# Moving the normalising steps by one step in an attention kernel on Trainium2, and giving its second head the values-in-the-array form

## The chip, the cores and the metric

The kernel runs on one core of one Trainium2 chip. The metric is device microseconds of one execution. The change is compared with the kernel before it, which took 1919.98 us (median of 3 runs, 1919.51 to 1921.93).

Engine names are those of the profile: PE is TensorE (PEld its weight loads), DVE is VectorE, ACT is ScalarE, POOL is GpSimd, SP is SyncE, which here issues DMAs.

## The reference, cut to what matters

```python
B, Sq, D = 1, 2048, 640;  H, Sk, Dh = 32, 2048, 192;  F = 1536
xn = layernorm(x)
q  = (xn @ wq) as 32 heads of 192
p  = softmax(q @ k_cache^T * Dh**-0.5)          # 2048 x 2048 for each head
s  = concat(p @ v_cache) @ wo
g  = silu((silu(xn @ w1) * (xn @ w3)) @ w2)
out = x + s * g
```

All operands are bf16. Almost all the work is attention: 32 heads, each with scores (contraction 192) and values (contraction 2048) for 2048 queries and 2048 keys.

## The kernel before, in words

**Heads, blocks, steps.** One head after another is computed. A head has four *blocks* of 512 queries (`qb` 0 to 3), a block has eight *steps* (`p` 0 to 7), and a step takes 256 keys (two tiles of 128). This text writes "step 3" for `p == 3`, and "block (3, 2)" for head 3, `qb` 2. `step` (line 755) writes one step into the program:

1. `scores` (549): matmuls into one PSUM tile `st` of 128x1024 floats. There are two such tiles (`ps_st`, line 183); the projections use them too.
2. `weights` (566): one ACT exponential reads `st` and writes half of `pT`, bf16. A `pT` tile holds two steps, and its pool `pp` has three buffers (line 176). A block needs four `pT` tiles, so the tile of steps 6 and 7 takes the buffer of steps 0 and 1 of the same block, and the tile of steps 0 and 1 of the next block that of steps 2 and 3.
3. Value matmuls, which lag behind: `parts` is a list from which each step pops some. From step 3 on, five parts stay in the list (line 777), so each step runs two parts of the step but one before it and the first part (`high(0)`) of the step just before it.
4. In step 1, `extra` (1010): the projection of the same block of the next head's queries (`project_chunk`, 366, PE), and its two casts out of PSUM, `qF` and `qA` (line 386).
5. `do_chores` (732) at the end of the step: the delayed pieces whose time has come on a step counter, in the order in which they were put there; then at most one piece of `lazy`, in the steps that `slots` names.

Program order is the order of each engine's queue for everything that is pinned, and all of this is.

**Two forms of a head.** Heads 2 to 30 are *quads* (`in_quads`, 158): every matmul is 64x64, four at a time in the four quarters of the array. In the values (`values_quads`, 634), the 64x64 of `vt` is the loaded operand and `pT` (512 queries) streams, so that the output comes out with its channels on the partitions. Heads 0, 1 and 31 use `values` (610) instead: `pT` is loaded and `vt`, with a column of ones, streams, 193 wide. There the row sums of the softmax come out of the matmul, and `evict` (589) adds and normalises.

**Row sums of a quad head.** They are made on DVE (`row_sums`, 676), from all four `pT` tiles of a block:
- `fours`: the sum of two `pT` tiles (128x2048). It is due two counts after steps 3 and 7, which puts it at the end of step 4 of the block and of step 0 of the next. It is called the *second-half sum* when it stands in step 0 (it sums steps 4 to 7 of the block before) and the *first-half sum* when it stands in step 4 (it sums steps 0 to 3).
- `join`, `fold`, `ends`: due at the end of step 2 of the next block; the last writes `e`, which a DMA turns into `eT`.
- `turned_sums` (710): due 6 counts after `ends` (line 701), that is at the end of step 0, two blocks after the one that it belongs to. Five DVE instructions: reduce `eT` to `rs`, its reciprocal, and three that normalise `ox` into `ostage`; `staged` then issues a store from the SP queue when both heads of a pair are in.

**Output additions.** The outputs of a block lie in four PSUM banks. `evict_quads` (660) runs in step 1 of the next block, after the exponential: ACT copies one bank (`oa`, 665), DVE adds the other (`ot`, 666), twice, and a DMA turns `ot` into `ox`. These additions free the banks.

**Bound steps.** The exponential needs a bound `nb` for each head. `fold_keys` (415: three DVE reductions over the keys), `column_lengths` (430: two DVE pieces of squares and one of roots) and `head_bound` (459: three small DVE operations and a POOL reduction over the partitions) are put into `lazy` in step 3 of a block (1025 to 1034) and taken out one by one in the steps of `slots` (736).

**SwiGLU.** In odd heads, `swiglu_chunk` (528) gives one tanh on ACT and two DVE operations for each block.

Behind head 31 lie the FFN output and the output projection, about 290 us, which the diff doesn't touch.

Of the kernel before, what the change touches and what calls it, by code (L numbers as in the profile page):

```python
# [30 lines left out]
def _kernel_impl(ctx, tc, A_x, A_k_cache, A_v_cache, A_wq, A_wo, B_w1, B_w3, B_w2, out):  # L31
    nc = tc.nc
    _, SQ, D = A_x.shape
    _, H, SK, dh = A_k_cache.shape
# [5 lines left out]
    NQB = SQ // 512  # L40
# [48 lines left out]
    def load_weights(h):  # L89
        keep = pin if h <= 3 else (lambda x: x)  # L90
        wsel = B_w1 if h % 2 == 0 else B_w3
        m = h // 2
        parts = ((A_wq[:, h * DH:h * DH + P], 0, 0, P), (wsel[:, m * PGW:(m + 1) * PGW], 1, 0, PGW),
                 (A_wq[:, h * DH + P:(h + 1) * DH], 1, PGW, P))
        if h == 0:
            wq = lnx.tile([P, 2, DC, P], BF16, name="wq0")

            def piece(part):
                w, t, c0, c1 = part
                pin(nc.sync.dma_start(out=wq[:, t, :, c0:c1], in_=w.rearrange("(c p) d -> p c d", p=P)))  # L100
            return dict(wq=wq, pieces=[lambda part=part: piece(part) for part in parts])
        else:
            wq = wqp.tile([P, 2 * DC, P], BF16, tag="wq")
            for w, t, c0, c1 in parts:
                keep(nc.gpsimd.dma_start(out=wq[ROWS[t], :, c0:c1], in_=w.rearrange("(s p) d -> p s d", p=DT)))
        return dict(wq=wq)
# [49 lines left out]
            set_ones(L)  # L156

    def in_quads(h):
        return 1 < h < H - 1

    def load_ahead(h, qb):
        if qb == 0:
            loads[h] = load_weights(h)
        elif qb == 1:
            loads[h].update(load_keys(h, hold=True))
            loads[h]["rest"].pop(0)()
        elif qb == 2:
            while loads[h]["rest"]:
                loads[h]["rest"].pop(0)()
            copy_keys(h, loads[h])  # L170
# [3 lines left out]
    with ExitStack() as actx:  # L174
# [495 lines left out]
        def later(wait, f, *a):  # L670
            chores.append((clock[0] + wait, f, a))

        def add(out, a, b):
            pin(nc.vector.tensor_tensor(out=out, in0=a, in1=b, op=ALU.add))  # L674

        def row_sums(hd, qb, p, w):
            sm = hd["sums"]

            def fours():
                t = aq["tree"].tile([P, 2, 1024], BF16, tag="tree", name="tree")  # L680
                a, b = sm["w"]
                sm["w"] = []
                add(t[:], a[:], b[:])
                sm["t"].append(t)

            def join():
                a, b = sm["t"]
                add(a[:], a[:], b[:])
                sm["t"].pop()

            def fold():
                t = sm["t"][0]
                add(t[:, 0, :], t[:, 0, :], t[:, 1, :])

            def ends():
                t = sm["t"].pop()[:, 0, :]
                e = aq["two"].tile([P, 512], BF16, tag="e", name="e")
                add(e[:], t[:, 0:512], t[:, 512:1024])
                eT = aq["two"].tile([P, 4, P], BF16, tag="eT", name="eT")
                pin(nc.sync.dma_start_transpose(out=eT[:], in_=e[:]))  # L700
                later(6 if in_quads(hd["h"] + 1) or qb < NQB - 1 else 9, turned_sums, hd, qb, eT)

            sm["w"].append(w)
            if p % 4 == 3:
                later(2, fours)
            if p == NPAIR - 1:
                for f in (join, fold, ends):
                    later(4, f)
# [23 lines left out]
        def do_chores(h, qb, p):  # L732
            for c in [c for c in chores if c[0] <= clock[0]]:
                chores.remove(c)
                c[1](*c[2])
            slots = (5,) if h % 2 and h > 1 else (5, 6) if h > 1 and qb % 2 == 0 else (5, 6, 7)
            if p in slots and lazy and lazy[0][0] <= clock[0]:
                _, f, a = lazy.pop(0)
                f(*a)
# [211 lines left out]
        def load_last():  # L951
            w = wqp.tile([P, 2 * DC, P], BF16, tag="wq", name="wl")
            for r, src in zip(ROWS, (B_w1, B_w3)):
                nc.gpsimd.dma_start(out=w[r, :, :], in_=src[:, FPIG:FPIG + P].rearrange("(s p) d -> p s d", p=DT))
            last.update(w=w, g=qp.tile([P, SQ], BF16, tag="qA", name="gl"), u=qfp.tile([P, SQ], BF16, tag="qF", name="ul"))
# [22 lines left out]
        for h in range(1, H):  # L978
            if h >= H // 2 and ffn_w_loads:
                ffn_w_loads.pop(0)()  # L980
            if h == 1:
                loads[3] = load_weights(3)
                while loads[2]["rest"]:
                    loads[2]["rest"].pop(0)()
            elif h + 2 == H:
                load_last()
            if h + 1 < H:
                start_head(h + 1)
            hd = heads[h]
            hd.update(sums=dict(w=[], t=[]), ox={})  # L990
            if h == 1:
                lengths = [2]
                todo = []
            elif h + 1 < H:
                lengths = [] if h % 2 else [h + 1] + [h + 2] * (h + 2 < H)
                todo = [h + 1]
            else:
                lengths = todo = []
            chunks = [[0], [1], [2], [3]] if h + 1 < H else [[0, 1], [2, 3], [], []]
            gated = []  # L1000
            for qb in range(NQB):
                post = []
                if (h, qb) == (H - 1, 2):
                    while chores:
                        clock[0] += 1
                        do_chores(h, qb, 2)
                    astack.close()
                    acc["hTp"] = fstack.enter_context(tc.tile_pool(name="hTp", bufs=2, side="right"))

                def extra():  # L1010
                    if h % 2 == 1:
                        for c in chunks[qb]:
                            gate = swiglu_chunk(h // 2, heads[h - 1]["qF"], hd["qF"], c)
                            gated.append(gate if hd["quads"] else gate())
                    quads = before["quads"] if qb == 0 else hd["quads"]
                    if h + 1 < H:
                        post.append(project_chunk(h + 1, qb, quads=quads, cast_low=nc.scalar.copy if hd["quads"] else None))
                    else:
                        post.append(hidden_last(qb, quads))

                for p in range(NPAIR):
                    step(hd, qb, p, extra if p == 1 else None)
                    if p == 4 and 1 < h < H - 2:
                        load_ahead(h + 2, qb)
                    if p == 3 and (h, qb) != (1, 0):
                        keys = todo or ([2] if (h, qb) == (1, 1) else [])
                        for k in keys:
                            lazy.extend(fold_keys(k))
                        for k in lengths[:1] if qb % 2 == 0 or h == 1 else []:
                            lazy.extend(column_lengths(k))  # L1030
                            lengths = lengths[1:]
                        for k in keys:
                            lazy.append((0, head_bound, (k,)))
                        todo = []
                    if (h, qb, p) == (1, 0, 7):
                        copy_keys(2, heads[2]["L"])
                        loads[3].update(load_keys(3))
                    if (h, qb, p) == (1, 2, 7):
                        copy_keys(3, loads[3])
                    if h + 1 < H:  # L1040
                        if p == 3 and gated:
                            if hd["quads"]:
                                later(1, lambda f=gated.pop(0): gated.append(f()))
                            later(3, lambda: gated.pop(0)())
                    else:
                        if p > 4 and gated:
                            gated.pop(0)()
                        if p == 3:
                            gated.append(post.pop()())
            while lazy:  # L1050
                _, f, a = lazy.pop(0)
                f(*a)
                assert 0, "late"
            heads.pop(h - 1, None)
            before["quads"] = hd["quads"]
# [143 lines left out]
    with ExitStack() as dctx:  # L1199
# [32 lines left out]
        todo = [lambda qb=qb, j=j: parts.append(load_part(pools, qb, j)) for qb in range(LB) for j in range(4)][3:]  # L1232
# [177 lines left out]
```

## Time and profile before

| what | value |
|---|---|
| median of 3 runs | 1919.98 us (1919.51 to 1921.93) |
| the profiled execution, its own time | 1919.95 us |
| span of that execution in the profile | 1918.4 us |
| PE busy | 1911.2 us, 100% of the span |
| DVE busy | 1426.2 us, 74% |
| ACT busy | 1382.2 us, 72% |
| POOL busy | 160.0 us, 8% |
| granted TensorE clock | 1.0 |

The profile has a page (busy time of each engine, the span in 40 slices, the chain of work that ended last, the costliest groups of instructions) and a trace that can be asked for a timeline, for waits, and for busy time in chosen windows. In a timeline a row gives the start and the length in us, engine, line of the kernel, operation, tiles written and read, how many instructions were merged into the row, and in brackets the idle time before it and what ended it. Ends of matmuls are modelled: each shows about 0.38 us, while the next group of four starts 0.216 us after it. So PE's busy share says little; starts say more.

### The profile page before, as it was taken

What the parts mean: (1) busy time and instruction counts of PE and PEld (TensorE: products, weight loads), DVE (VectorE), ACT (ScalarE), POOL (GpSimd) and SP (SyncE); (2) the same over time, 40 slices, a digit from 0 to 9 for tenths busy, and PEclk for the clock granted to TensorE, in tenths of its full rate; (3) what the DMA queues carried; (4) which work ended last, traced back from release to release, by engine and by line L of the source; (5) the groups of instructions that cost most, each with busy time, mean ns of one, the idle gap of its engine ahead of it and who ended that gap; (6) DMA issues with size and microseconds to landing.
All of it is one profiled execution on the core that took longest, in us unless ns stands there. A gap on an engine that the chain in (4) does not pass through costs nothing.

```text
span 1918.4 us, 68912 instructions
## 1 busy us (share of the span) xinstructions
PE 1911.2 (100%) x30919; PEld 1201.9 (63%) x30919; DVE 1426.2 (74%) x2558; ACT 1382.2 (72%) x1521; POOL 160.0 (8%) x308
## 2 busy tenths in 40 slices
PE   9999999999999999999999999999999999999999
PEld 5665555566666666666666666666666666454456
DVE  8658888888888888888888888888888885521111
ACT  7778888888888888888888888888888887210000
POOL 3300100000000000010000000101000000000000
PEclk9999999999999999999999999999999999999999
DMA  8735656666665656666656565656666634937673
GB/s 170 151 73 101 138 108 129 115 122 113 119 127 113 127 104 126 108 126 119 129 105 133 103 129 101 138 96 139 106 131 113 124 60 125 272 82 156 159 151 76
DMA packets 598955, 235.86 MB, mean 123 GB/s; under 512 B 523312, under 2 KB 588304, under 8 KB 598656
## 3 DMA queue, kind: packets, MB, share of 16 engines
q1 hardware_dynamic: 585712, 201.80, 54.1%
q0 software_dynamic: 8256, 24.58, 4.9%
q8 instruction: 242, 3.96, 0.9%
q10 hardware_dynamic: 4688, 5.05, 0.9%
q14 instruction: 57, 0.47, 0.1%
HBM read 54.26 MB, written 31.98 MB: 45 GB/s over the span
## 4 chain that ended last, share of the span: by engine, by line
PE 98%; DMA 0%; DVE 0%; SPq 0%; ACT 0%; POOL 0%; issue 0%
PE st L562 34%; PE obank L641 31%; PE ps L363 14%; PE ps_s L1154 8%; PE obank L621 3%; PE ps_s L1110 3%; PE ps_f L1174 2%; PE ps_gu L941 1%; PE ps_f L1190 1%; PE ps L348 0%; DMA eT<-e 0%; DMA KT<-in_A_k_cache_dram 0%; DVE tree L674 0%; SPq L116 0%; PE ps_gu L348 0%; SPq L100 0%
## 5 line engine op out<-in xcount | busy, mean ns | idle before, releaser
L570 ACT ACTIVATE pT<-st,nb 128x1024 bf16<-128x1024 f32 x1016 | 1125.2, 1113 | 188.7 <-PE st L562 152.5
L641 PE MATMUL obank<-pT,vt 64*64 64x512 bf16 x11136 | 778.4, 376 | 0.2 <-DVE ot L666 0.2
L641 PEld LDWEIGHTS <-vt 64*64 64x64 bf16 x11136 | 397.5, 107 | 221.6 <-issue 0.8
L562 PE MATMUL st<-qS,KM 64*64 64x512 bf16 (+1 forms) x1951 | 410.4, 376 | 0.4 <-POOL qS L393 0.4
L562 PE MATMUL st<-qA,KT 64*64 64x512 bf16 (+1 forms) x1951 | 410.3, 376 | 0.0
L562 PE MATMUL st<-qD,KT 64*64 64x512 bf16 (+1 forms) x1951 | 410.3, 376 | 0.0
L562 PE MATMUL st<-qA,KM 64*64 64x512 bf16 (+1 forms) x1951 | 391.3, 376 | 0.0
L562 PE MATMUL st<-qS,KT 64*64 64x512 bf16 (+1 forms) x1951 | 391.2, 376 | 0.1
L562 PE MATMUL st<-qF,KT 64*64 64x512 bf16 (+1 forms) x1951 | 391.2, 376 | 0.0
L562 PEld LDWEIGHTS <-KT 64*64 64x64 bf16 (+1 forms) x7808 | 274.9, 106 | 150.8 <-issue 0.6
L363 PE MATMUL ps<-xnT,wq 64*64 64x512 bf16 (+1 forms) x2390 | 291.1, 376 | 0.0
L363 PE MATMUL ps<-xnS,wq 64*64 64x512 bf16 (+1 forms) x2390 | 287.9, 376 | 0.0
L674 DVE TENSOR_TENSOR tree<-pT,pT 128x2048 bf16<-128x2048 bf16 x232 | 282.7, 1218 | 3.2 <-ACT pT L570 3.2
L363 PEld LDWEIGHTS <-wq 64*64 64x64 bf16 (+1 forms) x4780 | 167.4, 107 | 98.0
L674 DVE TENSOR_TENSOR tree<-tree 128x2048 bf16<-128x2048 bf16 x232 | 221.2, 954 | 4.0
L666 DVE TENSOR_TENSOR ot<-oa,obank 128x512 bf16<-128x512 f32 x232 | 148.9, 683 | 84.7 <-ACT oa L665 84.2
L562 PEld LDWEIGHTS <-KM 64*64 64x64 bf16 (+1 forms) x3904 | 144.8, 106 | 62.9 <-issue 1.2
L1154 PE MATMUL ps_s<-oT,wo_sb 128*128 128x512 bf16 x720 | 155.7, 379 | 0.0
L714 DVE TENSOR_REDUCE rs<-eT 128x4 f32<-128x512 bf16 x116 | 79.1, 681 | 60.3 <-DMA eT<-e 59.4
L1154 PEld LDWEIGHTS <-wo_sb 128*128 128x128 bf16 x720 | 70.4, 98 | 84.9 <-issue 0.2
L665 ACT COPY oa<-obank 128x512 f32<-128x512 f32 x232 | 123.6, 589 | 0.0
L386 ACT CAST qF<-ps 128x512 bf16<-128x512 f32 x123 | 72.1, 587 | 60.1 <-PE ps L363 60.1
(160 smaller groups left out, 1433.0 us busy)
## 6 DMA issues: line engine op xcount, KB each, us to landing
o_scr<-ostage SPq DMA_DIRECT2D x64, 384.0 KB, 3.4
vt<-in_A_v_cache_dram SPq DMA_DIRECT2D x62, 384.0 KB, 5.1
qS<-qA SPq DMA_DIRECT2D x240, 64.0 KB, 2.1
qD<-qF SPq DMA_DIRECT2D x120, 64.0 KB, 3.1
KM<-KT SPq DMA_DIRECT2D x60, 128.0 KB, 5.1
wo_sb<-in_A_wo_dram POOLq DMA_DIRECT2D x1, 7680.0 KB, 32.2
wq<-in_A_wq_dram POOLq DMA_DIRECT2D x31, 160.0 KB, 3.5
hT_scr<-hblk SPq DMA_DIRECT2D x16, 256.0 KB, 3.0
```

The costliest lines, as they stand in the source:

```text
L363: pin(nc.tensor.matmul(halves[t][c, :], lhsT=w[ROWS[t], s, c], rhs=xs[ROWS[t], s // 2, qs], start=(s == 0), stop=(s == 2 * DC - 1)))
L386: pin(c(out=dst[:, qs], in_=src))
L562: pin(nc.tensor.matmul(st2[c, t * 512:(t + 1) * 512], lhsT=k[:, c], rhs=q[ROWS[t], qs], start=(s == 0), stop=(s == 2)))
L570: pin(nc.scalar.activation(out=pT2, in_=st2[:], func=ACT.Exp, scale=SCALE, bias=nb[:]))
L621: pin(nc.tensor.matmul(acc["o"][b][:, r, (j % 2) * 256:(j % 2) * 256 + DH + 1], lhsT=pT2[ROWS[r], t * 512 + j * P:t * 512 + (j + 1) * P], ...
L641: pin(nc.tensor.matmul(acc["o"][low][ROWS[c], r, :], lhsT=vt[ROWS[r], u, p, c0:c0 + DT], rhs=pT2[ROWS[r], u * 512:(u + 1) * 512], start=(p ...
L665: pin(nc.scalar.copy(out=oa[:], in_=bank[:, 0, :]))
L666: pin(nc.vector.tensor_tensor(out=ot[:, k * 512:(k + 1) * 512], in0=oa[:], in1=bank[:, 1, :], op=ALU.add))
L674: pin(nc.vector.tensor_tensor(out=out, in0=a, in1=b, op=ALU.add))
L714: pin(nc.vector.tensor_reduce(out=rs[:], in_=eT[:], axis=AX.X, op=ALU.add))
L1110: pin(nc.tensor.matmul(ps, lhsT=oT[:, k, :], rhs=wo_sb[:, k, c0:c1], start=(k == 0), stop=(k == OC - 1)))
L1154: pin(nc.tensor.matmul(ps_of[d], lhsT=wo_sb[:, k, d * P:(d + 1) * P], rhs=part(k // KQ)[:, k % KQ, :], start=(k == 0), stop=(k == OC - 1)))
```

## The change

- `in_quads` takes in head 1: its scores, values and projections take the 64x64 form, its outputs go through `evict_quads` and `row_sums`, and it needs no ones in `vt`. Its projections of head 2 cast `qF` on ACT.
- `turned_sums` is due 7 counts after `ends`, in place of 6: at the end of step 1, not of step 0. In step 1 the additions of `evict_quads` and the casts of `extra` are already in the program by then. (For the last block of head 30 it stays 9.)
- `slots`: in odd heads from 3 on, the one piece of `lazy` is taken in step 4 instead of step 5. In head 1 it is steps 5, 6, 7 of block 0, steps 5, 6 of block 1, and step 4 of blocks 2 and 3.
- The bound pieces for head 2 are put into `lazy` in block (1, 0), no longer in (1, 1).
- Head 1 keeps its tanh where it was.

```diff
     def in_quads(h):
-        return 1 < h < H - 1
+        return 0 < h < H - 1
...
-                later(6 if in_quads(hd["h"] + 1) or qb < NQB - 1 else 9, turned_sums, hd, qb, eT)
+                later(7 if in_quads(hd["h"] + 1) or qb < NQB - 1 else 9, turned_sums, hd, qb, eT)
...
-            slots = (5,) if h % 2 and h > 1 else (5, 6) if h > 1 and qb % 2 == 0 else (5, 6, 7)
+            slots = ((5, 6, 7), (5, 6), (4,), (4,))[qb] if h == 1 else (4,) if h % 2 else (5, 6) if qb % 2 == 0 else (5, 6, 7)
...
             if h == 1:
-                lengths = [2]
-                todo = []
+                lengths = todo = [2]
...
-                            gated.append(gate if hd["quads"] else gate())
+                            gated.append(gate if hd["quads"] and h > 1 else gate())
...
-                    if p == 3 and (h, qb) != (1, 0):
-                        keys = todo or ([2] if (h, qb) == (1, 1) else [])
+                    if p == 3:
+                        keys = todo
...
                         if p == 3 and gated:
-                            if hd["quads"]:
+                            if hd["quads"] and h > 1:
                                 later(1, lambda f=gated.pop(0): gated.append(f()))
                             later(3, lambda: gated.pop(0)())
```

## The prediction

> **What bounds the kernel now.** I read the page first: the chain that ended last, then the costliest groups.
>
> ```profile
> PE 1911.2 (100%) x30919; PEld 1201.9 (63%) x30919; DVE 1426.2 (74%) x2558; ACT 1382.2 (72%) x1521; POOL 160.0 (8%) x308
> ...
> PE 98%; DMA 0%; DVE 0%; SPq 0%; ACT 0%; POOL 0%; issue 0%
> ...
> L570 ACT ACTIVATE pT<-st,nb 128x1024 bf16<-128x1024 f32 x1016 | 1125.2, 1113 | 188.7 <-PE st L562 152.5
> L641 PE MATMUL obank<-pT,vt 64*64 64x512 bf16 x11136 | 778.4, 376 | 0.2 <-DVE ot L666 0.2
> ```
>
> 98% of the chain is PE, and the value matmuls in quads waited 0.2 us in all. PE stands still nowhere; a change can save only matmul time, or the rare stall, while it can lose wherever something now hidden comes late. So I looked next at what PE would wait for. The waits that touch the edited pieces:
>
> ```profile
> DVE ot L666 <- ACT oa L665: 84.2, 91, 1.8
> ...
> DVE rs L714 <- DMA eT<-e: 59.4, 63, 2.7
> ...
> PE obank L641 <- DVE ot L666: 0.2, 1, 0.2
> ```
>
> DVE stands in `turned_sums` for `eT` 63 times, and that can make the output additions late. But it cost PE once. These 59.4 us are idle time of an engine off the chain.
>
> Then the timeline of DVE in block (3, 3), which stands for all quad blocks:
>
> ```profile
> 210.33 0.67 DVE L714 TENSOR_REDUCE rs<-eT 128x4 f32<-128x512 bf16 x1
> 211.03 0.18 DVE L716 RECIPROCAL rl_all<-rs 128x4 f32<-128x4 f32 x1
> 211.25 0.69 DVE L719 TENSOR_TENSOR ostage<-ox,rl_all 128x512 bf16<-128x512 bf16 x1
> 211.85 0.29 DVE L722 TENSOR_TENSOR ox<-ox 128x256 bf16<-128x256 bf16 x1
> 212.18 0.43 DVE L723 TENSOR_TENSOR ostage<-ox,rl_all 128x256 bf16<-128x256 bf16 x1
> 212.52 1.22 DVE L674 TENSOR_TENSOR tree<-pT,pT 128x2048 bf16<-128x2048 bf16 x1
> 215.02 1.28 DVE L666 TENSOR_TENSOR ot<-oa,obank 128x512 bf16<-128x512 f32 x2 [1.28 <-ACT oa L665]
> 216.60 0.69 DVE L386 CAST qA<-ps 128x512 bf16<-128x512 f32 x1 [0.30 <-ACT qF L386]
> 217.21 1.94 DVE L674 TENSOR_TENSOR tree<-tree 128x2048 bf16<-128x2048 bf16 x2
> 219.19 0.43 DVE L674 TENSOR_TENSOR e<-tree 128x512 bf16<-128x512 bf16 x1
> 219.53 1.22 DVE L674 TENSOR_TENSOR tree<-pT,pT 128x2048 bf16<-128x2048 bf16 x1
> ...
> 221.88 0.42 DVE L543 TENSOR_TENSOR hblk<-pa,qF 64x512 bf16<-64x512 bf16 x1
> ```
>
> The order is: `turned_sums` (210.33 to 212.52), second-half sum (212.52), output additions (215.02), cast `qA`, join and fold, `e`, first-half sum (219.53). Idle time stands in two places only, 1.28 us ahead of the additions and 0.30 us ahead of `qA`, both spent waiting for ACT. From `qA` to the end of the first-half sum, 219.53 + 1.22 = 220.75, DVE runs without a gap.
>
> What waits for that sum? The tile of steps 6 and 7 takes the buffer of steps 0 and 1, which the first-half sum reads, so the exponential of step 6 may not start before it is over. ACT and PE in the same block:
>
> ```profile
> 222.03 1.11 ACT L570 ACTIVATE pT<-st,nb 128x1024 bf16<-128x1024 f32 x1
> ...
> 222.46 0.38 PE L562 MATMUL st<-qS,KM 64*64 64x512 bf16 x1
> ...
> 222.90 0.38 PE L562 MATMUL st<-qF,KT 64*64 64x512 bf16 x1
> 223.10 0.82 PE L641 MATMUL obank<-pT,vt 64*64 64x512 bf16 x12
> 223.75 0.38 PE L562 MATMUL st<-qS,KM 64*64 64x512 bf16 x1
> ```
>
> 222.03 is step 6's exponential, ending at 223.14. 222.46 is step 7's first score matmul, 223.75 the next block's. Between them stand three groups of values, the first at 223.10; with (223.75 - 223.10) / 3 = 0.217 for a group, the third, `high(0)` of step 6, starts at 223.53. It is the first reader of what the exponential wrote.
>
> That the wait exists is borne out by its extra instruction on ACT's queue, one for every second exponential (a `pT` tile holds two):
>
> ```profile
> L570 ACTq EVENT_SEMAPHORE  x505: 17/17/38, 28.8 to 1625.5; - x169
> ```
>
> **The slack.** Hand-overs: the scores end at 222.90 + 0.38 = 223.28 and the exponential that reads them starts at 223.32 (row below), so 0.04 to 0.05; for the sum to ACT I take 0.08, since that extra instruction of 0.02 lies between (estimates). ACT's slack: 222.03 - 220.75 - 0.08 = 1.20. PE's: 223.53 - 223.14 - 0.05 = 0.34. Together 1.54 us.
>
> ```profile
> 223.32 1.11 ACT L570 ACTIVATE pT<-st,nb 128x1024 bf16<-128x1024 f32 x1 [0.18 <-PE st L562]
> ```
>
> **The change, part by part.**
>
> *`turned_sums` at the end of step 1.* Its five instructions now stand behind the additions and, since step 1 casts before its chores, behind `qA`; ahead of join, fold, `e` and the first-half sum. They take from 210.33 to 212.52, 2.19 us. What they leave is of no use: the second-half sum may go earlier and DVE idles longer ahead of the additions, since these wait for ACT's copy, which follows step 1's exponential. The additions stay at 215.02, `qA` at 216.60. Behind `qA` the row has no gap to swallow anything, so the first-half sum ends at 220.75 + 2.19 = 222.94, the exponential starts at 223.02 and ends at 224.13, and PE resumes at 224.18 in place of 223.53: **0.65 us of stall in the block**, which is 2.19 - 1.54.
>
> Does the next block make it up? No: PE has no slack to hurry with. Does it grow? Behind the first-half sum DVE has the bound piece and SwiGLU, in the row up to 222.30; moved by 2.19 that is 224.49, and step 7's exponential, which the next second-half sum needs, then ends at about 224.13 + 1.11 = 225.24. So DVE has caught up, and each block starts as the one before. The even heads have the same spacing from the additions to the first-half sum, 232.06 - 227.54 = 4.52 against 219.53 - 215.02 = 4.51:
>
> ```profile
> 227.54 1.29 DVE L666 TENSOR_TENSOR ot<-oa,obank 128x512 bf16<-128x512 f32 x2
> ...
> 232.06 1.22 DVE L674 TENSOR_TENSOR tree<-pT,pT 128x2048 bf16<-128x2048 bf16 x1
> ```
>
> How many blocks? Those with both a `turned_sums` and a first-half sum: all 116 of heads 2 to 30, and blocks 2 and 3 of head 1: 118. **118 x 0.65 = +76.7 us.** Bounds of the 0.65: with both hand-overs at 0.04 the slack is 1.59 and the stall 0.60; with both doubled (0.16 and 0.10) it is 1.41 and 0.78. So +71 to +92.
>
> The moved piece also issues a store on SP's queue in odd heads. It now stands behind the moves of `qD` and `qS` (issued behind `qA`) and ahead of `eT`'s transfer, which waits for `e` anyway. `e` is 2.19 later, `eT` is read a whole step later in the following block but one, so the 63 waits go, worth nothing on PE.
>
> *The late additions.* The one wait, in block (15, 0):
>
> ```profile
> 779.00:782.00 3.00, 2.76 (x52) 1.51 (x47) 3.00 (x5) 1.70 (x2) 0.00 (x0) 1.00 0.02 3
> ```
>
> PE is idle for 0.24 us; two gaps, each hidden for 0.38 - 0.216 = 0.16 by the modelled ends, make it up to 0.56. **-0.5.**
>
> *Head 1 in quads.* Windows over head 1 and head 3, from the first score matmul to the next head's:
>
> ```profile
> 72.87:123.56 50.69, 50.69 (x788) 34.58 (x786) 29.75 (x67) 39.15 (x38) 5.82 (x14) 1.00 0.46 107
> ...
> 173.68:223.75 50.07, 50.07 (x932) 27.95 (x928) 42.34 (x68) 43.06 (x49) 4.45 (x8) 1.00 0.56 110
> ```
>
> PE is full in both, and head 3 is 0.62 shorter: **-0.6**. DVE's 29.75 rises to about head 3's 42.34 plus `column_lengths`, ACT's 39.15 to 43.06 (`qF`'s cast among it); 50.07 - 42.34 = 7.7 is left on DVE. If that cover went, the sums of head 1 would push its exponentials as above, which the 118 blocks hold already. The memset of ones leaves POOL, which is idle nearly throughout: 0.
>
> *Bound pieces.* Odd heads take theirs in step 4, not 5. On DVE nothing stands between the two places (the first-half sum ahead, SwiGLU's product behind), so the order stays; 0. But the last one, before an even head, inherits the 2.19: POOL's reduction
>
> ```profile
> 221.37 0.72 POOL L514 PARTITION_ALL_REDUCE nb<-ns  x1 [0.40 <-DVE ns L511]
> ...
> 224.70 2.33 ACT L570 ACTIVATE pT<-st,nb 128x1024 bf16<-128x1024 f32 x2 [0.26 <-PE st L562]
> ```
>
> would end at 222.09 + 2.19 = 224.28, and its reader at 224.70 moves to 225.35. A margin of 1.07: 0 here, and a rival below. Head 2's pieces have a block more: 0.
>
> **Sum**, against the execution's own 1919.95 (span 1918.4 and 1.55 around it; the median of the runs, 1919.98, is the same): 1919.95 + 76.7 - 0.5 - 0.6 = 1995.5. I forecast 1995.5 us, 3.9% slower. A measurement of this kernel can tell about 0.2%, or 3.8 us, from no change.
>
> **The rivals.**
>
> *Covered (not slower).* The five instructions fit somewhere: the push on the first-half sum is under 1.54 us, or they come to lie elsewhere in DVE's order than I read (then the change doesn't do what its name says). For it: DVE is idle 8 of 50 us in head 3, and today no exponential shows a wait for the sums. Against it: that idle time stands ahead of the additions, and what is moved comes after them; 2.19 would have to shrink by 0.65, with nothing in the row to shrink it. It decides at 1.54 us. Price: 1919.95 - 0.6 - 0.5 = 1918.9. Chance 0.14; within it, a gain over 0.2% has no source, since PE has no idle time to give: 0.01 for that.
>
> *The bound, too.* If POOL's reduction really ends over 1.07 us after its row does, each even head from 4 to 30 (14 of them) starts late on top. Bounded by the push, 14 x 2.19 = 31: up to 2026; half of it is 2011. For it: rows of POOL are rough. Against it: today the margin is 224.70 - 222.09 = 2.6 and nothing waits. Chance 0.05.
>
> *The clock.* A pause in every block could cost granted clock. If one step of each block, 223.75 - 222.46 = 1.29 us, then ran at half rate, 118 x 1.29 = 152 more: 2148. Against it: the clock reads 1.00 in the window around the one stall of this trace (779 to 782). Chance 0.02. [...]
>
> **How the numbers follow.** Forecast 0.79, covered 0.14, bound 0.05, clock 0.02. Predicted time: 1995.5. The range takes +71 to +92 of the forecast (1990 to 2011), widens it below to a push a tenth smaller (2.19 x 0.9 - 1.54 = 0.43, +51, 1970), and reaches half the bound's price, 2011, above; covered and the clock are left out: 1970 to 2012. Slower by over 0.2%: 0.79 + 0.05 + 0.02 = 0.86. Within 0.2%: 0.13. Faster: 0.01.
>
> **What would show it.** A quad block is 13.17 us long, not 12.52. In each, one exponential (step 6's) waits for DVE's `tree`, and a group of `obank` matmuls for ACT's `pT`: 118 of each. DVE's wait for `eT` is gone, and its wait for `oa` ahead of the additions is longer, 1.8 us or so. DVE's rows stand as additions, `qA`, `rs` to `ostage`, join. Head 1 without a `turned_sums` (blocks 0 and 1) is at 12.52. Wrong would be: blocks of 12.52 with `turned_sums` between `qA` and join (there is slack that I haven't seen), or `turned_sums` at another place.

## The result and the profile after

The changed kernel takes **1999.85 us** (median of 6 runs, 1999.54 to 2000.43) against 1919.74 us before in the same measurement: 1.0416 times as long, 95% interval 1.0402 to 1.0429. Forecast were 1995.5 us and 3.9%. The profiled execution took 1999.54 us, its span is 1998.0 us.

The page of the changed kernel: busy times, the chain that ended last, and three of the costliest groups.

```profile
PE 1933.6 (97%) x31063; PEld 1240.5 (62%) x31063; DVE 1444.5 (72%) x2570; ACT 1380.2 (69%) x1533; POOL 173.8 (9%) x307
...
PE 50%; DVE 36%; ACT 11%; issue 2%; SPq 0%; DMA 0%; POOL 0%; ACTq 0%
...
L570 ACT ACTIVATE pT<-st,nb 128x1024 bf16<-128x1024 f32 x1016 | 1117.3, 1112 | 272.0 <-PE st L562 114.2
L641 PE MATMUL obank<-pT,vt 64*64 64x512 bf16 x11520 | 834.4, 377 | 58.5 <-ACT pT L570 58.5
...
L666 DVE TENSOR_TENSOR ot<-oa,obank 128x512 bf16<-128x512 f32 x240 | 154.2, 684 | 200.2 <-ACT oa L665 200.2
```

DVE's share of the span fell, from 74% to 72%, and yet DVE now has 36% of the chain, which was 98% PE before. The busy share says nothing about this; the chain and the waits do. The waits of the changed kernel (total us, times, longest):

```profile
DVE ot L666 <- ACT oa L665: 200.2, 120, 1.8
...
ACT pT L570 <- DVE tree L674: 91.6, 87, 1.2
...
PE obank L641 <- ACT pT L570: 58.5, 118, 0.8
...
ACT pT L570 <- DVE ss L446: 18.0, 15, 1.2
ACT pT L570 <- DVE km L478: 13.9, 15, 1.2
```

PE waits 118 times for an exponential, once in each block that the forecast counted. ACT's waits for DVE stand in three rows, because the wait is put down to the instruction of DVE that was last seen: 87 + 15 + 15 = 117; the 118th, in block (20, 2), is put down to PE's scores. The wait for `eT` is gone. That for `oa` has grown from 84.2 us in 91 waits to 200.2 us in 120, so from 0.9 to 1.7 us each; the forecast was 1.8 or so (the longest, 1.8, was as long before).

DVE, ACT and PE in block (3, 2) of the changed kernel:

```profile
207.56 1.28 DVE L666 TENSOR_TENSOR ot<-oa,obank 128x512 bf16<-128x512 f32 x2 [1.81 <-ACT oa L665]
209.15 0.69 DVE L386 CAST qA<-ps 128x512 bf16<-128x512 f32 x1 [0.30 <-ACT qF L386]
209.76 0.68 DVE L714 TENSOR_REDUCE rs<-eT 128x4 f32<-128x512 bf16 x1
...
211.61 0.43 DVE L723 TENSOR_TENSOR ostage<-ox,rl_all 128x256 bf16<-128x256 bf16 x1
211.95 1.94 DVE L674 TENSOR_TENSOR tree<-tree 128x2048 bf16<-128x2048 bf16 x2
213.93 0.42 DVE L674 TENSOR_TENSOR e<-tree 128x512 bf16<-128x512 bf16 x1
214.27 1.22 DVE L674 TENSOR_TENSOR tree<-pT,pT 128x2048 bf16<-128x2048 bf16 x1
```

```profile
213.58 1.10 ACT L570 ACTIVATE pT<-st,nb 128x1024 bf16<-128x1024 f32 x1
215.58 2.12 ACT L570 ACTIVATE pT<-st,nb 128x1024 bf16<-128x1024 f32 x2 [0.91 <-DVE tree L674]
```

```profile
215.63 0.63 PE L641 MATMUL obank<-pT,vt 64*64 64x512 bf16 x8
216.75 0.41 PE L641 MATMUL obank<-pT,vt 64*64 64x512 bf16 x4 [0.49 <-ACT pT L570]
216.96 0.37 PE L562 MATMUL st<-qS,KM 64*64 64x512 bf16 x1
```

`rs` to `ostage` stand between `qA` and join, without a gap; the first-half sum ends at 214.27 + 1.22 = 215.49; step 6's exponential starts at 215.58, 0.91 us after ACT was free; and the third group of values starts at 216.75, where 215.63 + 2 x 0.216 = 216.06 would have been its time. The stall is 0.69 us, and 216.96 is the start of the next block, 13.20 us after this one's.

### The profile page after: what moved, and what is told of

The parts are those of the page before. It is cut to its first block, busy times and chain, and to the rows that moved or that the text cites. A ratio compares the mean times of both kernels' runs of the same rounds, so it can differ in the third digit from the quotient of the medians.

```text
span 1998.0 us, 69263 instructions
## 1 busy us (share of the span) xinstructions
PE 1933.6 (97%) x31063; PEld 1240.5 (62%) x31063; DVE 1444.5 (72%) x2570; ACT 1380.2 (69%) x1533; POOL 173.8 (9%) x307
## 4 chain that ended last, share of the span: by engine, by line
PE 50%; DVE 36%; ACT 11%; issue 2%; SPq 0%; DMA 0%; POOL 0%; ACTq 0%
DVE tree L674 17%; PE ps L363 14%; PE st L562 10%; PE obank L641 9%; PE ps_s L1153 8%; ACT pT L570 7%; DVE ostage L719 4%; DVE qA L386 4%; DVE rs L714 4%; ACT qF L386 4%; PE ps_s L1109 3%; DVE e L674 2%; DVE ostage L723 2%; PE obank L621 2%; PE ps_f L1173 2%
## 5 line engine op out<-in xcount | busy, mean ns | idle before, releaser
L641 PE MATMUL obank<-pT,vt 64*64 64x512 bf16 x11520 | 834.4, 377 | 58.5 <-ACT pT L570 58.5
L641 PEld LDWEIGHTS <-vt 64*64 64x64 bf16 x11520 | 437.2, 107 | 305.2 <-issue 94.7
L562 PE MATMUL st<-qD,KT 64*64 64x512 bf16 (+1 forms) x1983 | 417.5, 376 | 0.0
L562 PE MATMUL st<-qA,KT 64*64 64x512 bf16 (+1 forms) x1983 | 417.3, 376 | 0.0
L562 PEld LDWEIGHTS <-KT 64*64 64x64 bf16 (+1 forms) x7936 | 289.6, 107 | 137.1 <-issue 0.6
L674 DVE TENSOR_TENSOR tree<-pT,pT 128x2048 bf16<-128x2048 bf16 x240 | 292.7, 1220 | 26.9 <-ACT pT L570 23.3
L666 DVE TENSOR_TENSOR ot<-oa,obank 128x512 bf16<-128x512 f32 x240 | 154.2, 684 | 200.2 <-ACT oa L665 200.2
L363 PEld LDWEIGHTS <-wq 64*64 64x64 bf16 (+1 forms) x4860 | 176.8, 107 | 89.6
L674 DVE TENSOR_TENSOR tree<-tree 128x2048 bf16<-128x2048 bf16 x240 | 229.1, 955 | 4.1
L386 DVE CAST qA<-ps 128x512 bf16<-128x512 f32 x120 | 82.9, 691 | 36.9 <-ACT qF L386 36.9
```

What stands on the lines that cost most here:

```text
L363: pin(nc.tensor.matmul(halves[t][c, :], lhsT=w[ROWS[t], s, c], rhs=xs[ROWS[t], s // 2, qs], start=(s == 0), stop=(s == 2 * DC - 1)))
L386: pin(c(out=dst[:, qs], in_=src))
L562: pin(nc.tensor.matmul(st2[c, t * 512:(t + 1) * 512], lhsT=k[:, c], rhs=q[ROWS[t], qs], start=(s == 0), stop=(s == 2)))
L641: pin(nc.tensor.matmul(acc["o"][low][ROWS[c], r, :], lhsT=vt[ROWS[r], u, p, c0:c0 + DT], rhs=pT2[ROWS[r], u * 512:(u + 1) * 512], start=(p ...
L666: pin(nc.vector.tensor_tensor(out=ot[:, k * 512:(k + 1) * 512], in0=oa[:], in1=bank[:, 1, :], op=ALU.add))
```

## The experiments

Every kernel below was compared with the kernel before, on the same chip. "A" is the theory of the prediction: the five instructions of `turned_sums` push the first-half sum by 2.19 us, step 6's exponential must wait for it because it takes a `pT` buffer that the sum reads, and PE stalls for what is over the slack. B, C, D and E are its rivals, as the expectations name them.

| kernel | time, us | before, us | ratio, 95% interval | quad blocks, us |
|---|---|---|---|---|
| changed | 1999.85 | 1919.74 | 1.0416 (1.0402 to 1.0429) | 13.20 |
| changed, 6 counts | 1920.02 | 1919.98 | 1.0000 (0.9991 to 1.0009) | 12.52, four late |
| before, 7 counts | 1998.73 | 1919.98 | one run | 13.21 |
| changed, four `pT` buffers, room from `osp`, `hbp` | 1932.78 | 1919.98 | 1.0066 (1.0050 to 1.0081) | 12.52 |
| changed, four `pT` buffers, room from `ot`, `e` | 1918.11 | 1919.54 | 0.9991 (0.9982 to 1.0000) | 12.52 |
| changed, 11 counts | 1918.22, 1918.01 | 1919.98, 1919.58 | 0.9992 (0.9983 to 1.0001), twice | 12.52 |
| changed, two instructions ahead | 1918.07 | 1919.54 | 0.9990 (0.9981 to 1.0000) | 12.52 |
| changed, four instructions ahead | 1945.83 | 1919.54 | one run | 12.75 |
| changed, 9 counts | 1999.13 | 1919.58 | one run | 13.2 |
| before, 11 counts | 1919.32 | 1919.54 | 0.9998 (0.9989 to 1.0007) | 12.52 |
| before, odd heads' step 4 | 1919.65 | 1919.58 | 1.0001 (0.9991 to 1.0010) | 12.52 |

**One edit at a time: the position or the rest?** The changed kernel with only the position undone:

```diff
-                later(7 if in_quads(hd["h"] + 1) or qb < NQB - 1 else 9, turned_sums, hd, qb, eT)
+                later(6 if in_quads(hd["h"] + 1) or qb < NQB - 1 else 9, turned_sums, hd, qb, eT)
```

> The changed kernel with turned_sums due 6 counts after ends again (end of step 0); head 1 stays in quads, the bound steps stay respread. Theory A (the five instructions behind the additions push the first-half sum, and step 6's exponential waits for it because of the pT buffer): no push, so all blocks are back at 12.52 us and the time is 1918.9 us, perhaps plus the 0.2 that block (1, 0) lost. Theory B (head 1's new form or the respread bound steps cost the time, or part of it): over 1930, up to 1999.9. No exponential waits for the sums by A.

And the kernel before with only the position changed (6 to 7 in the same line):

> The kernel before with the one number changed: 7 counts in place of 6. Head 1 stays as it was. Theory A: 114 blocks (all of heads 2 to 30 but the first two of head 2, which have no turned_sums) each 0.69 us longer, 78.2 us, less 0.5 for the one late addition: 1997.5 us. Theory B: at most a few us over 1919.7.

1920.02 and 1998.73 us. The position alone makes the whole loss; head 1's new form and the respread steps, without it, make no difference that the interval shows. B falls. In the first, A's 1918.9 was missed by 1.1: with 6 counts the additions are sometimes late, and four blocks of that profile stall. Its DVE waits for `eT` as before:

```profile
DVE rs L714 <- DMA eT<-e: 68.5, 64, 2.6
```

In the second, PE's waits are the 114 that were counted:

```profile
PE obank L641 <- ACT pT L570: 57.2, 114, 0.7
```

The odd heads' bound steps by themselves (`(4,)` in place of `(5,)` in the kernel before):

> The kernel before with odd heads' bound step in step 4 in place of step 5, nothing else. The order of DVE and of SP is the same to the instruction; on POOL only a copy and the memset of ones before the last head change places. Theory A: no change, 1919.6 us, within 0.1%. If the respread steps carry a gain or a loss of their own, over 1 us either way.

1919.65 us: nothing, as the unchanged order of DVE said.

**Is it the buffer, or is DVE full?** A fourth `pT` buffer takes away what the exponential waits for and leaves DVE as it is.

```diff
-        pp = actx.enter_context(tc.tile_pool(name="pp", bufs=3))
+        pp = actx.enter_context(tc.tile_pool(name="pp", bufs=4))
...
-        osp = actx.enter_context(tc.tile_pool(name="osp", bufs=2))
+        osp = actx.enter_context(tc.tile_pool(name="osp", bufs=1))
...
-        hbp = actx.enter_context(tc.tile_pool(name="hbp", bufs=2))
+        hbp = actx.enter_context(tc.tile_pool(name="hbp", bufs=1))
```

> The changed kernel with four pT buffers in place of three; to make room, the pools osp and hbp have one buffer each instead of two. DVE's order and load stay those of the changed kernel. Theory A: step 6's exponential then takes the buffer of steps 6 and 7 of the block before, whose sum was over long ago; the stall goes though the first-half sum still ends at 11.73 us of its block, and the time is about 1919. Theory C (DVE has become the bound: with the idle time ahead of the additions it has no room for its work in 12.52 us): the blocks stay near 13.2 us and the time near 2000, since DVE has as much to do in the same order.

1932.78 us: neither 1919 nor 2000. Blocks were 12.52 us from (1, 1) to the end of head 30, as A has it, but head 31 had two long gaps. The waits of this kernel name where they come from:

```profile
ACT pt L536 <- DVE pa L541: 12.3, 2, 6.7
PEld L621 <- ACT pT L570: 11.5, 5, 5.8
```

A tanh of SwiGLU (`pt`) waited for DVE's product to free a tile of `hbp`, the pool that I had cut to one buffer; the exponentials stood behind it in ACT's queue, and PE behind them. That is an error of the experiment. Taking the room elsewhere settles it:

```diff
-            ot = aq["two"].tile([P, 1024], BF16, tag="ot", name="ot")
+            ot = aq["one"].tile([P, 1024], BF16, tag="ot", name="ot")
...
-                e = aq["two"].tile([P, 512], BF16, tag="e", name="e")
+                e = aq["one"].tile([P, 512], BF16, tag="e", name="e")
```

> The changed kernel with four pT buffers again, but the room comes from ot and e, with one buffer each (each is written once in a block and read by a DMA within some 5 us), not from osp and hbp. Theory A: as in the first try the quad blocks are 12.52 us, and head 31 now goes at its old pace, with no gap of PE over 1 us: about 1918.5 us. If the 14 us over that the first try showed came from the fourth buffer itself and not from hbp's single buffer, they come again: 1932 us.

1918.11 us. DVE and ACT of this kernel in a block of head 3:

```profile
203.86 0.69 DVE L386 CAST qA<-ps 128x512 bf16<-128x512 f32 x1 [0.30 <-ACT qF L386]
204.47 0.68 DVE L714 TENSOR_REDUCE rs<-eT 128x4 f32<-128x512 bf16 x1
...
208.99 1.22 DVE L674 TENSOR_TENSOR tree<-pT,pT 128x2048 bf16<-128x2048 bf16 x1
```

```profile
208.23 3.47 ACT L570 ACTIVATE pT<-st,nb 128x1024 bf16<-128x1024 f32 x3
```

The first-half sum starts 208.99 - 203.86 = 5.13 us after `qA`, as in the changed kernel (214.27 - 209.15 = 5.12), and ends at 210.21. ACT doesn't care: three exponentials from 208.23 to 211.70 in a row, right through that time. Same order on DVE, same lateness, no loss. C falls, and the buffer is the link.

**Is there a threshold?** `turned_sums` cut in two: the first n of its five instructions in step 1, the rest, with the store, in step 5 (`later(4, rest)`). Two ahead:

```diff
-            pin(nc.vector.tensor_reduce(out=rs[:], in_=eT[:], axis=AX.X, op=ALU.add))
...
+            for f in ops[:2]:
+                f()
+            later(4, rest)
```

> The changed kernel with turned_sums cut in two: its first two instructions (reduce, reciprocal) at the end of step 1 as in the change, the other three at the end of step 5. Theory A has a threshold: the two push the first-half sum by 0.71 + 0.21 = 0.92 us, under the 1.54 us of slack, so nothing is lost: 1918.2 us, the time of the kernel with 11 counts. Theory D (each microsecond put between the additions and the first-half sum costs PE in proportion: 81 us for 2.19, no threshold): 1918.2 + 34 = 1952 us.

And four ahead (`ops[:4]`):

> The same cut, with four instructions at the end of step 1 and only the last at the end of step 5. The push is 0.71 + 0.21 + 0.61 + 0.32 = 1.85 us. Theory A: 1.85 - 1.50 (the slack as the changed kernel's 0.69 of stall gives it, 2.19 - 0.69) = 0.35 us of stall in each of 118 blocks: 1918.2 + 41 = 1959 us, blocks of 12.87 us. Theory D: 1918.2 + 81 x 1.85 / 2.19 = 1987 us, blocks of 13.10 us.

1918.07 and 1945.83 us. Two ahead cost nothing, so there is a threshold, and D falls. Their push was a little less than was expected: by DVE's rows of that kernel, 205.24 - 204.43 = 0.81 us from `rs` to join, not 0.92.

```profile
204.43 0.68 DVE L718 TENSOR_REDUCE rs<-eT 128x4 f32<-128x512 bf16 x1
205.15 0.18 DVE L719 RECIPROCAL rl_all<-rs 128x4 f32<-128x4 f32 x1
205.24 1.92 DVE L674 TENSOR_TENSOR tree<-tree 128x2048 bf16<-128x2048 bf16 x2
```

Four ahead cost less than A's figure, for the same reason: the push was mis-sized. DVE of that kernel:

```profile
205.23 0.69 DVE L386 CAST qA<-ps 128x512 bf16<-128x512 f32 x1 [0.30 <-ACT qF L386]
205.84 0.68 DVE L718 TENSOR_REDUCE rs<-eT 128x4 f32<-128x512 bf16 x1
...
207.38 0.28 DVE L722 TENSOR_TENSOR ox<-ox 128x256 bf16<-128x256 bf16 x1
207.58 1.94 DVE L674 TENSOR_TENSOR tree<-tree 128x2048 bf16<-128x2048 bf16 x2
```

From `rs` to join are 207.58 - 205.84 = 1.74 us, not 1.85. The time lost is (1945.83 - 1918.1) / 118 = 0.235 us in a block, which leaves 1.74 - 0.235 = 1.50 of slack; the changed kernel's figures leave 2.19 - 0.69 = 1.50. Between the two, 0.45 us more of push is 0.45 us more of stall. So the threshold lies between 0.81 and 1.74 us by these runs, and at 1.50 if the stall grows as the push does from there on.

**Another place ahead of the sum, and one behind it.** 9 counts put `turned_sums` behind `e`, but still ahead of the first-half sum:

> The changed kernel with 9 counts: turned_sums at the end of step 3, behind join, fold and e, but still ahead of the first-half sum. Theory A: the push on the first-half sum is the same 2.19 us, so the time is again about 1999.5 us, with blocks of 13.20 us, though e is back at its old place. Theory E (the cost comes through the late join, fold or e and its transfer on SP's queue): about 1918.2 us.

1999.13 us, again with 118 waits of PE. So the late join, fold and `e` have no part in it, and E falls. 11 counts put it behind the first-half sum:

> The changed kernel with turned_sums due 11 counts after ends: end of step 5, behind the additions and behind the first-half sum. Theory A: the first-half sum is back at 9.54 us of its block, nothing waits for it, the additions are never late: 1918.9 us, the shortest of all by some tenths. Theory C: DVE still idles ahead of the additions and has the same work, so the blocks stay longer than 12.52 us; if its work then runs into the next second-half sum, the time is between 1930 and 2000.

1918.22 us. DVE of this kernel in a block of head 3:

```profile
203.77 0.69 DVE L386 CAST qA<-ps 128x512 bf16<-128x512 f32 x1 [0.30 <-ACT qF L386]
204.38 1.94 DVE L674 TENSOR_TENSOR tree<-tree 128x2048 bf16<-128x2048 bf16 x2
206.35 0.42 DVE L674 TENSOR_TENSOR e<-tree 128x512 bf16<-128x512 bf16 x1
206.69 1.22 DVE L674 TENSOR_TENSOR tree<-pT,pT 128x2048 bf16<-128x2048 bf16 x1
207.83 1.21 DVE L419 TENSOR_REDUCE mk<-KT 128x1 f32<-128x1024 bf16 x1
208.96 0.68 DVE L714 TENSOR_REDUCE rs<-eT 128x4 f32<-128x512 bf16 x1
```

Behind `turned_sums` only SwiGLU's two operations stand in this block ahead of the next second-half sum, and the waits of this kernel show none of PE for them. The additions are never late, `eT` is never waited for. A's 1918.9 was 0.7 too much; most of that lies in the last store (below). Once more, for the interval, and with head 1 in its old form (the kernel before with 11 for 6):

> The 11-count kernel once more, for the interval: 1918.2 us, 0.999 of the kernel before, by A; if its first result was chance, 1.000.

> The kernel before with the one number changed to 11 counts; head 1 keeps its old form. The position alone: the late output additions go (0.5 us in the trace of before, about 1 in that of the 6-count kernel), head 1's 0.4 to 0.5 us aren't gained: 1918.7 us, between before and the 11-count kernel with head 1 in quads. If head 1's form is worth nothing or less, it is as fast as that one, 1918.2 us.

1918.01 and 1919.32 us; the second was forecast at 1918.7. No order tried is shorter than 11 counts (two instructions ahead and the second four-buffer kernel are as short). It is about 0.08% under the kernel before in both measurements, but the upper end of its interval is 1.0001, so the times alone don't prove a gain. The profiles agree with one: from the first score matmul of head 3 to head 31's there are 1402.67 us before and 1402.05 us in 11-count kernels with either form of head 1, so the late additions had cost 0.6. Head 1 in quads is 50.28 us in place of 50.69.

A further 0.7 us lies behind the last matmul. There the last store of the output landed 1.45 us after its issue in the changed kernel, and 2.21 us after it in the kernel before. The two 11-count kernels differ in head 1's form and in where the bound steps stand (which by themselves changed nothing), and their spans (1917.7 with the old form, 1916.7 and 1916.5 in quads) by 1.0 to 1.2 us, of which head 1 itself is 0.4. So this difference seems to go with the form of head 1 (an estimate from the spans), though that store comes 1.8 ms behind head 1 and is the same in both; why is open.

## Why the prediction was right, step by step

**The order on DVE**: right. `turned_sums` stood behind `qA`, ahead of join: nothing delayed it, and it delayed everything behind it. The chain of the changed kernel goes through exactly these rows, from the projection over `qF`, `qA`, `rs`, `ostage`, `tree` to `pT` and `obank`.

**The link to ACT**: right, and shown by the fourth buffer.

**118 blocks**: right, by PE's 118 waits.

**0.65 us in each**: mis-sized by 0.04. Between the changed and the 11-count kernel lie 1998.0 - 1916.7 = 81.3 us of span, 0.69 for each of 118, not 76.7. The push was the 2.19 of the forecast; the slack was 1.50, not 1.54, and both of its parts were a little off. The hand-overs were estimated at 0.08 and 0.05; they are 215.58 - 215.49 = 0.09 from the sum to the exponential, and 0.05 from the exponential to the values, 0.15 together by the unrounded times in place of 0.13. The two distances that they are taken from, 1.28 and 0.39, are 1.67 together in the model block, and 1.65 in the median of all blocks of heads 2 to 30, in the kernel before as in the changed kernel with 11 counts. 1.65 - 0.15 = 1.50.

**Head 1 in quads, -0.6**: it was -0.4 in head 1 itself (50.69 to 50.28). The forecast took head 3 as the model, but block (1, 0) is 0.2 longer than a quad block. About 0.04 of it goes with the passage from one form of matmul to the other, as in head 2 before (12.56 us for its first block, 12.52 for the next). The rest, 0.16, the change made itself: the projection's `qF` is now cast on ACT, behind the tanh (77.58 to 78.21), so the cast `qA` on DVE comes late, and the next scores wait for the PSUM tile that it frees. These are the rows of the 11-count kernel; the score group starts at 79.45 in place of 78.63 + 3 x 0.216 = 79.28.

```profile
78.63 0.82 PE L641 MATMUL obank<-pT,vt 64*64 64x512 bf16 x12
78.71 0.69 DVE L386 CAST qA<-ps 128x512 bf16<-128x512 f32 x1 [1.20 <-ACT qF L386]
...
79.45 0.37 PE L562 MATMUL st<-qS,KM 64*64 64x512 bf16 x1
```

**Late additions, -0.5**: -0.6.

**Not in the sum at all**: the last store, -0.7. With it the terms close: 81.3 - 0.4 - 0.6 - 0.7 = 79.6, which is 1998.0 - 1918.4. The forecast came out 4 us short because of the stall's 4.6; this unforeseen gain hid part of that.

**Rivals.** *Covered* was decided where the forecast put it, at a push of 1.5 us: 0.81 by its rows (two ahead) is free, and 1.74 (four ahead) costs. *The bound, too*: in none of the even heads from 4 to 30 did ACT wait for POOL's `nb`. At head 4 of the changed kernel the reduction ends at 229.98 and its reader starts at 231.13, a margin of 1.15 where 1.07 was forecast. *The clock*: 1.00 in the changed kernel throughout, with a pause of 0.69 us in each of 118 blocks.

## What to carry to other kernels

An engine that is 74% busy and has 0% of the chain may still have a deadline in every block. Work that is moved on it must be followed to the next release of a buffer behind it, not only to the wait that the move is to shorten: here a wait that cost PE 0.6 us in all was taken away, and a release with 1.50 us of slack was passed by 2.19. Such slack shows in no view of waits, since nothing waits yet; it has to be added up from a timeline, hand-over by hand-over, up to the engine that is the bound.

If a piece is off the path, try it behind the last release of its block: here it cost nothing there (11 counts), and 81 us just ahead of that release (7 and 9 counts).

## What the runs showed of the hardware that I had not expected

**A pause of 5.62 us was followed by half the clock; pauses of 0.69 us weren't.** In the kernel with one `hbp` buffer, PE stood still for 5.62 us in head 31. Its busy time in windows around that (columns: stretch, length, then busy time of PE, PEld, DVE, ACT, POOL, granted clock, DMA share, GB/s), and the first score matmuls behind it:

```profile
1580.00:1583.30 3.30, 3.30 (x58) 2.01 (x52) 3.23 (x7) 0.88 (x2) 0.00 (x0) 1.00 0.30 55
1583.30:1589.20 5.90, 0.30 (x8) 0.07 (x2) 5.48 (x10) 1.66 (x3) 0.00 (x0) 0.87 0.19 36
1589.20:1590.20 1.00, 0.98 (x10) 0.71 (x12) 0.13 (x1) 1.00 (x2) 0.00 (x0) 0.50 0.00 0
1590.20:1593.20 3.00, 3.00 (x26) 1.76 (x24) 1.12 (x2) 1.60 (x2) 0.00 (x0) 0.50 0.02 5
1593.20:1596.00 2.80, 2.80 (x42) 2.02 (x40) 0.00 (x0) 1.51 (x2) 0.00 (x0) 0.77 0.00 0
```

```profile
1589.84 0.63 PE L562 MATMUL st<-qS,KM 64*128 64x512 bf16 x1
...
1590.27 0.63 PE L562 MATMUL st<-qA,KT 64*128 64x512 bf16 x1
```

Whole windows stand at 1.00 or at 0.50. If a figure between them is the mean of a window with both, the clock was already 0.50 for the last 1.5 us of the pause (0.87 over 5.90 us), and stayed there for 1.00 + 3.00 + 1.3 us (0.77 over 2.80 us) of PE's work; the 1.5 and the 1.3 are estimates from these rows. In that time there were 1590.27 - 1589.84 = 0.43 us from group to group in place of 0.216.

In the changed kernel the clock read 1.00 through the 118 pauses of 0.69 us. What a pause between 0.69 and 5.62 us would do, these rows don't show.

**On DVE an instruction that doesn't read what the one before wrote started 0.12 to 0.13 us sooner in these rows.** Behind the 128x256 addition `ox`, the normalising that reads it starts 212.18 - 211.85 = 0.33 us later in the kernel before; join, which doesn't read it, starts 207.58 - 207.38 = 0.20 us later in the four-ahead kernel. The rows of block (3, 3) before show the same on other pairs. The reciprocal, which reads `rs`, starts 0.03 us behind that row's end (210.33 + 0.67, then 211.03); the second-half sum, which doesn't read `ostage`, starts 0.09 us ahead of that row's end (212.18 + 0.43, then 212.52). That difference of 0.12 us is why four instructions pushed by 1.74 us and not by 1.85, and two by 0.81 and not by 0.92.
